# Forming half of a block's weight-gradient products inside the attention forward loop instead of after it

## The chip, the cores and the metric

One Trainium2 chip, one core. The metric is the device time of one execution in microseconds (us). Every version below is correct, except one that is wrong and says so. A program on one core can't be compared with a neighbouring die, so an execution counts as "fast" when it lies within 1.5% of the fastest of the same kernel.

Engines: PE multiplies matrices, DVE and ACT work on vectors, POOL (GpSimd) does some of the elementwise work, SP only issues DMA transfers. SPq is SP's instruction queue. "L351" is a line of that kernel's own file, so the same statement has another line number in another kernel.

## The reference, cut to what matters

A transformer block with adaptive layer norm (2048 tokens, width 512, 32 heads of 16, hidden width 1792), its output and the gradients of nine inputs. Three weight gradients are products over all tokens:

```python
h = _layernorm(x) * (1 + ca) + sa
x = x + ga * attention(h, wqkv) @ wo             # O = attention(...)
h = _layernorm(x) * (1 + cb) + sb                # h2
r = relu(h @ w1 + b1); s = r * r
out = x + gb * (s @ w2 + b2)
# backward, with g = grad_out, gf = g * gb:
# dW2 = s^T gf      dW1 = h2^T dz      dWo = O^T da        (sums over 2048 tokens)
```

The 2048 tokens are four chunks of 512, so each gradient is a sum of four parts, one for each chunk.

## The kernel before

The attention forward pass is a loop of 512 "units": four score products, two exponentials on ACT, one every 0.92 us (945.9 us busy for 1024), four products with V. A unit can't be shorter than its exponentials, about 1.83 us. Chunk c of the dense part (forward and backward of the MLP) is a coroutine. It starts when the heads of its 512 tokens are done and does one small step in each later unit. Chunk 3 has no units left, so it runs after the loop, in the "last stage". There too all weight gradients are formed: "early" products from data of chunks 0 to 2 that were stored to DRAM, then "late" products from chunk 3. The attention backward pass follows.

```python
def load_wB(transposed):                       # (cut)
    w = ffw.tile([P, FC, D], BF, name="wB", tag="wB")
    if transposed:
        for fc in range(FC):                   # 14 transposing loads of w1
            SP.dma_start(out=w[:, fc, :], in_=B_w1[:, fc*P:(fc+1)*P], transpose=True)
    else: ...                                  # one load of w2

def dense_chunk(c, O_c, act):                  # act: chunk 3
    w1_nat = load_wA(False); w1T = load_wB(True)
    g_c = ...; SP.dma_start(out=g_c[:], in_=g_dram[:, ts, :])
    x1_c = ...; SP.dma_start(out=x1_c[:], in_=x_dram[:, ts, :])
    OT = ...;  SP.dma_start(out=OT..., in_=flat(O_c), transpose=True)
    gf_c = ...; POOL.tensor_tensor(gf_c[:], g_c[:], gb_bc..., ALU.mult)
    gfT = ...; SP.dma_start(out=gfT..., in_=flat(gf_c), transpose=True)
    yield 6                                    # wait six units
    for ti in range(4): ...                    # OT @ wo, layer norm   (cut)
    yield 10
    def to_tokens(key, src, f0, f1):           # s or dz, tokens on partitions
        tk = cb.tile([P, 3, 4, P], BF, name="tk", tag="tk", bufs=5)
        SP.dma_start(out=tk..., in_=flat(src[:, f0:f1, :]), transpose=True)
        if act: last[key].append(tk)
        else:   SP.dma_start(out=(s_st if key == "s" else dz_st)[c, f0//3][:, 0:nf], in_=tk[:, 0:nf])
    ...                                        # 14 steps h @ w1; load of w2^T; 14 steps ds   (cut)
    for ti in range(4):                        # gradient through w1: pdh
        for fc in range(FC):
            PE.matmul(pdh[:], dzT[:, fc, ti*P:(ti+1)*P], w1T[:, fc, :], ...)
            if fc % 4 == 3: yield 0
        ...                                    # layer-norm gradient on DVE, first half (cut)
        DVE.tensor_tensor(uq[:], dxn2[:], tq[:], ALU.subtract)        # second half
        DVE.scalar_tensor_tensor(out=dx1_c[:, ti, :], ...)
        DVE.tensor_tensor(proda[:], dx1_c[:, ti, :], a_c[:, ti, :], ALU.mult)
        DVE.tensor_tensor(da_c[:, ti, :], dx1_c[:, ti, :], ga_bc, ALU.mult)
        yield 0
    ...                                        # MLP output with w2; attention gradient (cut)

def fpv(u):                                    # in the forward loop
    ...
    if kt == TT - 1:                           # every 16th unit a group of heads ends
        DVE.tensor_copy(ostage[:], oacc[:])    # frees PE's one accumulator "oacc"

# last stage (cut): gradients
res = dwp["r"].tile([P, 512], BF, name="dwres", tag="dwres", bufs=2)
if nev[0] % 2 == 0: ACT.activation(res[:, 0:w], acc[:, 0:w], AF.Identity)
else:               DVE.tensor_copy(res[:, 0:w], acc[:, 0:w])
SP.dma_start(out=dst, in_=res[:, 0:w])

fill_steps(9)                                  # nine steps of gradient work ...
ffinish(*fdone.pop(0)[1:])                     # ... then O of chunk 3
for w in dense.pop(0): fill_steps(1 + w)       # one gradient step per step of chunk 3
for _ in fill: pass                            # what is left: the tail
```

PE, ACT and DVE run in program order in the forward loop.

## Time and profile before

| | us |
|---|---|
| median of 4 executions (2782.72 to 2788.53) | 2787.55 |
| preparation | to 111 |
| forward loop, 512 units | 111 to 1092.9 |
| last stage | 1092.9 to 1315.4 |
| attention backward, and what follows it | 1315.4 to 2786.6 |

The view of busy time by windows shows the bound. Its rows are the first 128 units without dense work, the units of chunks 0, 1 and 2, and the last stage. Columns: window, its length, busy us (and instruction count) of each engine, granted PE clock (1.00 is full), DMA share, GB/s.

```profile
core 0: us, PE busy (x) PEld busy (x) DVE busy (x) ACT busy (x) POOL busy (x), PEclk, DMA share, GB/s
111.10:344.00 232.90, 215.41 (x1016) 40.06 (x1015) 27.14 (x33) 232.90 (x256) 17.34 (x20) 0.50 0.49 127
344.00:592.00 248.00, 220.03 (x1284) 58.66 (x1280) 90.31 (x186) 234.56 (x255) 34.52 (x39) 0.77 0.37 93
592.00:840.00 248.00, 220.22 (x1286) 58.73 (x1283) 91.73 (x186) 235.77 (x256) 45.22 (x44) 0.77 0.44 106
840.00:1092.90 252.90, 223.37 (x1302) 59.30 (x1303) 92.50 (x186) 240.72 (x260) 45.23 (x44) 0.77 0.48 118
1092.90:1315.40 222.50, 184.06 (x887) 87.57 (x887) 89.15 (x192) 19.39 (x33) 52.29 (x44) 0.91 0.66 163
```

In the loop ACT is the bound: 232.9 of 232.9 us without a chunk, 235 of 248 with one. PE's 220 of 248 us look nearly full, but much of it is slow work: in the 233 us without dense work the granted clock was 0.50, in the chunks' units 0.77. The Trainium skill, "TensorE: Matmul & The Clock Gate", section "What's actually happening", says that the default state is half clock, and that sustained activity of about 3.4 us lifts it. The trace fits: where chunk 0's products begin, at 379 us, the granted clock was 0.50 to 382 us, 0.74 from 382 to 385 and 1.00 from 385 to 388. PE's records fill 215 of the 233 us at 0.50. The first two units after an empty stretch take up to 2.9 us each; they are called cold below. In the last stage PE is the bound, busy 184 of 222 us and idle for 38. (The last stage is counted to the first exponential of the attention backward.)

Three units, one in each chunk, take 6.4 us. The timeline of DVE, then of PE, shows the first (columns: start, duration, engine, line, operation, output and inputs, count, and in brackets the idle time before it with what ended it):

```profile
500.92 1.26 DVE L476 TENSOR_TENSOR uqb<-dxn,tqb 128x512 bf16<-128x512 bf16 x1
502.21 0.75 DVE L477 SCALAR_TENSOR_TENSOR dx_c<-uqb,rstd,g_c 128x512 bf16<-128x512 bf16 x1
503.07 0.43 DVE L480 TENSOR_TENSOR proda<-dx_c,a_c 128x512 bf16<-128x512 bf16 x1
503.53 0.42 DVE L481 TENSOR_TENSOR a_c<-dx_c,modbc 128x512 bf16<-128x512 bf16 x1
503.88 0.68 DVE L590 COPY ostage<-oacc 128x512 f32<-128x512 f32 x1
```

```profile
504.61 0.62 PE L586 MATMUL oacc<-ET,vaug 128*32 128x512 bf16 x4 [3.66 <-DVE ostage L590]
```

PE's next product with V needs the accumulator, and its copy stands behind four DVE operations of the gradient.

### The profile page before, as it was taken

The numbers are of one execution on the slowest core, as the hardware profiler recorded it, in microseconds if no ns is written. First come the engines' busy times: TensorE is split into PE (matmuls) and PEld (weight loads), VectorE is DVE, ScalarE is ACT, GpSimd is POOL, SyncE is SP. The second block draws the span as 40 slices with busy tenths as digits, with TensorE's granted clock in tenths as the row PEclk, the third lists the DMA queues.
The fourth block names the chain that finished last, engine by engine and source line by source line (L and its number), as shares of the span: only waits on it lengthen the run. The fifth ranks groups of instructions, "written<-read, shape, count | busy, mean of one in ns | idle before, by whom it ended". The sixth has DMA issues, their size and how long they took to land.

```text
span 2786.6 us, 47985 instructions
## 1 busy us (share of the span) xinstructions
PE 2453.4 (88%) x17994; PEld 790.8 (28%) x17994; DVE 1710.3 (61%) x2133; ACT 2301.8 (83%) x3531; POOL 366.6 (13%) x326
## 2 busy tenths in 40 slices
PE   6699998898889887799889889889988888989999
PEld 2111122222221222344232332323323233333243
DVE  7101133325333332453798998989889899898873
ACT  4599999999999996101798999989999999999953
POOL 2010010211212022122011010111101011010100
PEclk8655568867885887899799999999999999999999
DMA  8853316344434544784999999999999999999982
GB/s 239 218 153 79 100 48 145 91 120 99 107 95 103 120 128 119 201 191 128 200 190 190 190 189 193 187 189 192 189 187 194 195 189 196 188 186 213 179 249 80
DMA packets 1269550, 449.16 MB, mean 161 GB/s; under 512 B 1187763, under 2 KB 1240503, under 8 KB 1268806
## 3 DMA queue, kind: packets, MB, share of 16 engines
q1 hardware_dynamic: 1262854, 431.71, 77.4%
q10 hardware_dynamic: 6464, 14.40, 1.9%
q8 instruction: 141, 2.31, 0.3%
q14 instruction: 91, 0.75, 0.1%
HBM read 89.81 MB, written 62.94 MB: 55 GB/s over the span
## 4 chain that ended last, share of the span: by engine, by line
PE 39%; ACT 37%; DVE 7%; issue 6%; DMA 5%; SPq 2%; ACTq 0%; POOL 0%; DVEq 0%; POOLq 0%
ACT ET L572 17%; ACT E_u L954 15%; PE psS_u L952 10%; PE accVK L1006 3%; ACT dsT L1065 3%; PE accVK L997 2%; DVE dS_u L966 2%; DMA dsT<-dS_u 2%; PE psST L570 2%; PE pm L436 2%; PE pm L494 2%; PE ptT L987 2%; PE pm L419 2%; PE dqacc L1024 2%; PE dwa L822 2%
## 5 line engine op out<-in xcount | busy, mean ns | idle before, releaser
L966 DVE TENSOR_TENSOR dS_u<-psD_u,E_u 128x1024 bf16<-128x1024 f32 x1024 | 1196.7, 1217 | 145.1 <-PE psD_u L964 72.6
L954 ACT ACTIVATE E_u<-psS_u 128x512 bf16<-128x512 f32 x1790 | 989.3, 617 | 92.7 <-PE psD_u L964 65.0
L572 ACT ACTIVATE ET<-psST 128x1024 bf16<-128x1024 f32 x1024 | 945.9, 1293 | 37.8 <-PE psST L570 37.7
L952 PE MATMUL psS_u<-ik,iq 32*128 32x512 bf16 x1790 | 620.2, 389 | 102.0 <-ACT E_u L954 59.6
L570 PE MATMUL psST<-qt_sb,kt_sb 32*128 32x512 bf16 x2048 | 462.1, 505 | 78.9 <-ACT ET L572 32.1
L964 PE MATMUL psD_u<-iv,ido 32*128 32x512 bf16 x2048 | 410.2, 396 | 14.8 <-DVE dS_u L966 13.7
L586 PE MATMUL oacc<-ET,vaug 128*32 128x512 bf16 x2048 | 270.1, 517 | 13.8 <-DVE ostage L590 13.3
L590 DVE COPY ostage<-oacc 128x512 f32<-128x512 f32 x32 | 22.1, 690 | 351.9 <-PE oacc L586 324.7
L570 PEld LDWEIGHTS <-kt_sb 32*128 32x128 bf16 x2048 | 91.4, 95 | 455.8 <-issue 450.8
L952 PEld LDWEIGHTS <-iq 32*128 32x128 bf16 x2048 | 121.2, 91 | 344.3 <-issue 314.9
L997 PE MATMUL accVK<-dS_u,qz 128*32 128x512 bf16 x2048 | 210.8, 401 | 2.8 <-DVE dS_u L966 0.2
L1006 PE MATMUL accVK<-E_u,dOs_tok 128*16 128x512 bf16 x2048 | 207.3, 395 | 0.0
L1039 POOL TENSOR_TENSOR dQacc<-dQacc,dqtmp 128x512 f32<-128x512 f32 x64 | 81.3, 1270 | 890.8 <-ACT dqtmp L1034 890.8
L964 PEld LDWEIGHTS <-ido 32*128 32x128 bf16 x2048 | 104.8, 91 | 257.3 <-issue 255.0
L1024 PE MATMUL dqacc<-dsT,KS_tok 128*32 128x512 bf16 x2048 | 162.2, 395 | 11.4 <-ACT dsT L1065 11.4
L954 ACT ACTIVATE E_u<-psS_x 128x512 bf16<-128x512 f32 x258 | 159.3, 618 | 0.2 <-PE psD_u L964 0.2
L1065 ACT ACTIVATE dsT<-ptT 128x1024 bf16<-128x1024 bf16 x128 | 133.9, 1046 | 1.1 <-PE ptT L987 1.0
L783 ACT ACTIVATE dwres<-dwa 128x512 bf16<-128x512 f32 (+2 forms) x19 | 10.1, 530 | 132.8 <-DMA out_dram<-dwres 77.0
L586 PEld LDWEIGHTS <-vaug 128*32 128x32 bf16 x2048 | 55.8, 98 | 192.2 <-issue 192.2
L439 DVE SCALAR_TENSOR_TENSOR rT<-pm,rT 128x512 bf16<-128x512 f32 x56 | 38.6, 691 | 113.3 <-PE pm L436 112.2
L952 PE MATMUL psS_x<-ik,iq 32*128 32x512 bf16 x258 | 100.6, 390 | 0.0
L987 PE MATMUL ptT<-identb,dS_u 128*128 128x128 bf16 x1024 | 82.3, 226 | 11.8 <-ACT dsT L1065 11.6
(246 smaller groups left out, 2093.1 us busy)
## 6 DMA issues: line engine op xcount, KB each, us to landing
kt_sb<-qkT_st SPq DMA_DIRECT2D x128, 64.0 KB
wA<-in_B_w_dram SPq DMA_DIRECT2D x4, 1792.0 KB
wB<-in_B_w_dram SPq DMA_DIRECT2D x4, 1792.0 KB
dsT<-dS_u SPq DMA_TRANSPOSE x448
s_st<-tk SPq DMA_DIRECT2D x12, 384.0 KB
dz_st<-tk SPq DMA_DIRECT2D x12, 384.0 KB
slab<-s_st SPq DMA_DIRECT2D x12, 384.0 KB
slab<-dz_st SPq DMA_DIRECT2D x12, 384.0 KB
```

What stands on the lines that cost most here:

```text
L570: PE.matmul(ps[:, hi, :], kt_sb[r:r + 32, kt * P:(kt + 1) * P], qt_sb[r:r + 32, :], start=True, stop=True, tile_position=(r, 0))
L572: ACT.activation(ET[:, 2 * pair:2 * pair + 2, :], ps[:], AF.Exp, scale=SCALE)
L586: PE.matmul(oacc[32 * hq:32 * hq + 32, :], lhsT, ET[:, hq, :], start=(kt == 0), stop=(kt == TT - 1), tile_position=(0, 32 * hq), skip_grou ...
L952: PE.matmul(psS[:], st["q"][r:r + 32, qt * P:(qt + 1) * P], st["k"][r:r + 32, kc * 512:kc * 512 + 512], start=True, stop=True, tile_positi ...
L954: ACT.activation(bst[u][0][:, hq, :], psS[:], AF.Exp, scale=SCALE)
L964: PE.matmul(psD[:, hi, :], st["do"][r:r + 32, qt * P:(qt + 1) * P], st["v"][r:r + 32, kc * 512:kc * 512 + 512], start=True, stop=True, til ...
L966: DVE.tensor_tensor(dS_u[:, 2 * pair:2 * pair + 2, :], psD[:], E_u[:, 2 * pair:2 * pair + 2, :], ALU.mult)
L987: PE.transpose(pt[:, i, :], held["dS"][:, 2 * half + i // 4, kt * P:(kt + 1) * P], identb[:])
L997: PE.matmul(cur["vk"][32 * hq:32 * hq + 32, :], hst[hg]["qz"][:, qt, hq, :], bst[u][1][:, hq, :], start=(qt == 0), stop=False, tile_positi ...
L1006: PE.matmul(acc[32 * hq:32 * hq + DH, :], dOs_tok[:, qt, (hg * 4 + hq) * DH:(hg * 4 + hq + 1) * DH], E_u[:, hq, :], start=False, stop=(qt ...
L1024: PE.matmul(acc[32 * hq:32 * hq + 32, :], KS_tok[:, kc * 4 + kt, h * DH:h * DH + 32], tT[:, :, hq * 4 + kt, :], start=(kt == 0), stop=(kt ...
L1065: ACT.activation(dst, pt[:], AF.Identity)
```

## The change

Intent: the 456 early products need about 95 us of PE in the last stage. Chunks 0 and 1 are finished early enough to form their parts while the forward loop, bound by ACT, leaves PE room. Each part is a chain of four products into one PSUM bank, copied by DVE and stored to DRAM as fp32. Chunk 1's store adds to chunk 0's. Chunk 2's data are stored as before. The last stage loads the sums and adds them when it reads out its accumulators. Also, the second half of the layer-norm gradient of a tile is put off to after the fourth product of the next tile.

```diff
+        def add_chain(c, lag, idx, w, lhs, rhs):
+            def run():
+                acc = mm()
+                for ti in range(4):
+                    PE.matmul(acc[:, 0:w], lhs(ti), rhs(ti), start=(ti == 0), stop=(ti == 3))
+                part = cb.tile([P, 512], F32, name="part", tag="part", bufs=2)
+                DVE.tensor_copy(part[:, 0:w], acc[:, 0:w])
+                if c == 0:
+                    SP.dma_start(out=p_st[idx][:, 0:w], in_=part[:, 0:w])
+                else:
+                    POOL.dma_start(out=p_st[idx][:, 0:w], in_=part[:, 0:w], accum_op=ALU.add)
+            dwq.append((unit[0] + lag, run))
...  (dense_chunk, to_tokens)
+                elif key == "s":
+                    for f in range(nf):
+                        add_chain(c, 5, f0 + f, D, lambda ti, f=f: tk[:, f, ti, :], lambda ti: gf_c[:, ti, :])
...  (the same for dz and O; the gradient's second half becomes finish_dx)
+                    if fc == 3 and rest:
+                        rest.pop()()
...  (forward loop: chains alternate with steps of the chunk, or fill units in which it waits)
+            ripe = dwq and not open_group[0] and u >= dwq[0][0]
+            if wait > 0:
+                wait -= 1
+                if ripe:
+                    next_chain()
+                return
...
+            if ripe and turn:
+                turn = 0
+                next_chain()
+                return
...  (last stage)
                     res = dwp["r"].tile([P, 512], BF, name="dwres", tag="dwres", bufs=2)
-                    if nev[0] % 2 == 0:
-                        ACT.activation(res[:, 0:w], acc[:, 0:w], AF.Identity)
-                    else:
-                        DVE.tensor_copy(res[:, 0:w], acc[:, 0:w])
+                    DVE.tensor_tensor(res[:, 0:w], acc[:, 0:w], parts.pop(j)[:, 0:w], ALU.add)
+                    fetch_part(j + 6)
                     SP.dma_start(out=dst, in_=res[:, 0:w])
...
-                    for t in range(NL):          # 12 early products for each accumulator
+                    for t in range(4):           # now 4
```

## The prediction

> **What bounds the kernel now**, from the busy-by-window view and the timeline. (a) Forward loop, 111 to 1093 us, 512 units of two exponentials: ACT is 92 to 98 of every 100 us busy; a unit without dense work ends every 1.83 us. Chunk work costs more in few places: the first two units after an empty stretch last about 2.86 us with the granted clock near 0.50 (later ones about 1.87), and once per chunk a unit lasts 6.37 us because the copy of the head sum stands on DVE behind the layer-norm gradient. 128 units take 232.8 us without a chunk, 248 with one. (b) Last stage, 1093 to 1314 us: PE is busy 184 of 221 us; 456 early products take 95 us of PE. They interleave one group to one with chunk 3, and 35 us of products (1273 to 1308) follow after chunk 3 is done. (c) Attention backward from 1314: untouched.
>
> **What the change does.** Early products in the last stage fall from 456 to 152: about 63 us less PE (95 x 2/3). They return as 76 chains in the forward loop, each about 0.9 us of PE, a DVE copy of about 0.69 us and a store of 128 to 256 KB; chunk 1's stores accumulate and come from GpSimd (the Trainium skill, "DMA: Bandwidth & Descriptors", SWDGE vs HWDGE: accumulation only there; no run shows its cost yet). The last stage gains 38 loads of sums, and all 38 evacuations become DVE adds instead of 19 on each engine.
>
> **On the critical path.**
> - Forward: chains fall mostly into units whose dense work was waiting; the built order keeps 512 units. Warm chain units cost +0.03 us: +2. Filled gaps avoid about four cold starts of 2 us: -8. The deferred gradient and new alignment shorten the three 6.37 us units: -8 to -11. Against it: only two buffers for sums; in runs of 6 or 7 chains in successive units a store must land within about 3 us. Estimate +0.5 us per such unit for chunk 0, +1.5 for chunk 1: +5 to +20. Net about -6.
> - Last stage: the 35 us tail disappears and W2's products lose their interleave (-7). Chunk 3's own chain remains. Losses: the transpose of O now stands behind six sum loads and the slabs in the SP queue (+10 to 16, mostly repaid by the earlier start of chunk 3's loads); two result buffers make DVE wait for output stores inside chunk 3 (+5 to 8); the row sums are no longer hidden before the tail (+5). Net about -28.
>
> **Prediction:** 2754 us, 8 in 10 within 2722 to 2790. Faster by over 2%: 0.19; within: 0.77; slower: 0.04.
>
> **What would show it.** Forward loop ends within 15 us of 1093; chunk 1's 128 units longer than chunk 0's, DVE copies of sums waiting for DMA; fewer units at clock 0.5. In the last stage PE busy falls by about 60 us but the stage by only 25 to 35, PE idle at the transposed loads (O, h2, w2, da); backward takes the same time.
>
> **What would make it wrong.** Faster: stores land quickly, so the forward loop gains 15 us, and chunk 3, freed of interleaving, runs closer to its DMA chain. Slower: accumulating stores take 8 us or more and stall PE through the chains' single PSUM bank; the SP queue, longer by 76 transfers, delays keys or weights; backward starts later for lack of an operand.

## More of the kernel before

SP's queue is ordered by a scheduler, by what it believes is ready first; once built, the order is fixed.

What SP issued before chunk 1 (its timeline) turned out to matter most. These lines are one stretch of it, with other transfers left out:

```profile
584.97 18.09 SPq L336 DMA_TRANSPOSE wB<-in_B_w_dram  x14
...
615.87 3.87 SPq L363 DMA_TRANSPOSE gfT<-gf_c  x1
...
620.41 3.52 SPq L355 DMA_TRANSPOSE OT<-O_c  x1
```

The fourteen transposing loads of w1 hold SP for 18 us, but they lie between 585 and 603 us. At that time chunk 0 is over and chunk 1 has not begun: 24 units without dense work lie between two chunks (571.5 to 614.4 us on PE). The transpose of O goes out at 620.

In the last stage PE waits little for transfers (view of waits: who waits, for what, us in total, times, longest):

```profile
DVE dwres L785 <- DMA out_dram<-dwres: 27.3, 9, 8.0
...
PE pm L609 <- DMA rrows<-ostage: 10.2, 1, 10.2
...
PE pm L371 <- DMA OT<-O_c: 9.4, 1, 9.4
```

## The result, and the profile after

The changed kernel takes 2812.78 us (median of 4, 2808.77 to 2823.29), beside 2787.55 us before. The ratio is 1.010, 95% interval 1.007 to 1.013: 1% slower, and above the predicted range. Ratios here are the mean time of one kernel's fast runs over that of the other's in the same rounds, so not quite the ratio of the quoted medians.

The profiled execution of after was its slowest (2823 us). Busy time by windows, same rows as before:

```profile
111.20:344.00 232.80, 215.29 (x1016) 40.28 (x1015) 27.15 (x33) 232.80 (x256) 17.30 (x20) 0.50 0.47 124
344.00:593.00 249.00, 221.94 (x1384) 66.43 (x1380) 97.06 (x200) 234.56 (x256) 31.80 (x37) 0.86 0.39 92
593.00:862.00 269.00, 222.94 (x1433) 69.33 (x1431) 111.03 (x222) 236.52 (x256) 75.32 (x80) 0.87 0.59 108
862.00:1126.50 264.50, 219.06 (x1359) 62.37 (x1356) 106.39 (x213) 239.74 (x259) 50.40 (x49) 0.82 0.49 116
1126.50:1341.90 215.40, 134.51 (x583) 58.94 (x583) 97.56 (x211) 9.36 (x15) 53.38 (x45) 0.82 0.65 157
```

Chunk 0's units take as long as before. Those of chunks 1 and 2 take 21 and 12 us more. The forward loop ends at 1126.5 instead of 1092.9 us. The last stage has 50 us less of PE work and is only 7 us shorter: PE now idles 81 us in it instead of 38.

Taking the end of each unit's second exponential from the two traces and sorting the units by length gives the balance of the loop, as the excess over 1.833 us summed over the units of each class:

```
units                     before          after
2.4 to 3.2 us (cold)    29:  25.9 us    16:  15.1 us
over 3.2 us              3:  13.6 us    10:  56.1 us
the rest                      5.6 us          7.4 us
```

So the expected gains came: cold starts fell by 10.8 us, and none of the three 6.4 us units is left. The loss is ten new long units. They are two of 15.5 and 15.7 us (27.5 us over the floor together), six of 4.5 to 7.2 us in which a chain waits (22.5 us), and two others (6.1 us).

The two longest begin chunks 1 and 2. PE, then ACT, at the first (timeline):

```profile
646.14 1.89 PE L395 MATMUL pm<-wo_nat,OT 128*128 128x512 bf16 x4 [12.62 <-DMA OT<-O_c]
```

```profile
648.67 1.94 ACT L622 ACTIVATE ET<-psST 128x1024 bf16<-128x1024 f32 x2 [13.61 <-PE psST L620]
```

PE stands for 12.6 us before the first product with the transposed O; the scores behind it in PE's order are late, and ACT, the bound of the loop, is idle for 13.6 us. Why O is late, SP's timeline shows:

```profile
623.50 5.18 SPq L338 DMA_TRANSPOSE wB<-in_B_w_dram  x4
628.78 1.55 SPq L581 DMA_TRANSPOSE dOT<-dOs_c  x1
630.37 2.58 SPq L338 DMA_TRANSPOSE wB<-in_B_w_dram  x2
...
638.51 3.03 SPq L588 DMA_DIRECT2D d_st<-dltT  x4
641.66 1.77 SPq L378 DMA_TRANSPOSE OT<-O_c  x1
```

The w1 loads are no longer a block at 585 to 603 us. They run from 609.5 to 633 us, between chunk 0's last transfers, and the transpose of O goes out at 641.7. Chunk 0 now ends about when chunk 1's heads do, because its 38 chains took units. The loads wait for chunk 0's w2, whose tile they reuse (SP waits 6.2 us for PE just before them), so they can't start earlier. The 24 empty units that the chains filled had hidden 18 us of SP issue. (The Trainium skill, "Perfetto Trace Analysis", "DMA Instruction — HWDGE (DVE, Sync)", says that such a row ends when the sequencer is free, and that the movement of data is not in it. The trace agrees: this row ends at 643.4, PE goes on at 646.1.)

The waits that grew (view of waits over the whole span):

```profile
PE pm L395 <- DMA OT<-O_c: 46.5, 3, 21.1
...
DVE part L353 <- DMA p_st<-part: 43.1, 14, 5.9
...
DVE dwres L858 <- DMA out_dram<-dwres: 41.8, 20, 9.0
...
PE pm L351 <- DVE part L353: 20.2, 11, 4.5
...
PE dwa L896 <- DVE dwres L858: 15.7, 4, 5.7
...
PE pm L659 <- DMA rrows<-ostage: 15.6, 1, 15.6
...
PE pm L455 <- ACT h2T L415: 13.1, 1, 13.1
```

Line 2: DVE can't copy a sum because both buffers are still being stored, and in line 4 PE waits for that copy. Lines 3 and 5: the same in the last stage with two result buffers. Lines 1 and 6: the 21.1 us for chunk 3's O (9.4 before) and the 15.6 us for the last head's sums (10.2 before). Line 7: chunk 3's transposed h2. Before the change, early products filled this wait (PE ran them to 1147.6 us, when h2 came), and the view of before has no such line. Lines 3 and 5 need care. Before, the read-outs waited longer for output stores, 77.0 us on ACT and 27.3 us on DVE, but the view shows no wait of PE for a read-out. What grew, and what costs, is line 5.

The accumulating stores land like this (issues on POOL; view of one line's instructions):

```profile
L357 POOL DMA_DIRECT2D p_st<-part x38: 851/862/1071, 693.4 to 878.3; - x38
...
DMA to landing us min/median/max: 2.9/4.1/9.1
```

### The profile page after: what moved, and what is told of

Same layout as the page of the kernel before. It is cut to its first block, busy times and chain, and to the rows that moved or that the text cites. A ratio compares the mean times of both kernels' runs of the same rounds, so it can differ in the third digit from the quotient of the medians.

```text
span 2821.5 us, 48292 instructions
## 1 busy us (share of the span) xinstructions
PE 2410.4 (85%) x17994; PEld 783.3 (28%) x17994; DVE 1760.7 (62%) x2228; ACT 2291.6 (81%) x3512; POOL 398.7 (14%) x364
## 4 chain that ended last, share of the span: by engine, by line
PE 38%; ACT 31%; DVE 9%; DMA 8%; issue 6%; SPq 3%; POOL 1%; ACTq 0%; DVEq 0%; POOLq 0%
ACT E_u L1030 14%; ACT ET L622 12%; PE psS_u L1028 10%; PE accVK L1082 3%; ACT dsT L1141 3%; PE psST L620 3%; DVE dS_u L1042 3%; DMA dsT<-dS_u 3%; PE accVK L1073 2%; PE ptT L1063 2%; PE pm L455 2%; PE dqacc L1100 2%; PE pm L472 2%; DMA out_dram<-dwres 2%; PE oacc L636 2%
## 5 line engine op out<-in xcount | busy, mean ns | idle before, releaser
L620 PE MATMUL psST<-qt_sb,kt_sb 32*128 32x512 bf16 x2048 | 417.4, 476 | 65.2 <-ACT ET L622 27.5
L1040 PE MATMUL psD_u<-iv,ido 32*128 32x512 bf16 x2048 | 413.1, 399 | 13.9 <-DVE dS_u L1042 13.2
L636 PE MATMUL oacc<-ET,vaug 128*32 128x512 bf16 x2048 | 253.8, 485 | 7.4 <-DVE ostage L640 6.9
L353 DVE COPY part<-pm 128x512 f32<-128x512 f32 (+2 forms) x76 | 46.0, 605 | 94.8 <-PE pm L351 51.2
L1073 PEld LDWEIGHTS <-qz 128*32 128x32 bf16 x2048 | 55.2, 93 | 125.4 <-issue 123.4
```

Of the source, the lines that this page charges most:

```text
L620: PE.matmul(ps[:, hi, :], kt_sb[r:r + 32, kt * P:(kt + 1) * P], qt_sb[r:r + 32, :], start=True, stop=True, tile_position=(r, 0))
L636: PE.matmul(oacc[32 * hq:32 * hq + 32, :], lhsT, ET[:, hq, :], start=(kt == 0), stop=(kt == TT - 1), tile_position=(0, 32 * hq), skip_grou ...
L1040: PE.matmul(psD[:, hi, :], st["do"][r:r + 32, qt * P:(qt + 1) * P], st["v"][r:r + 32, kc * 512:kc * 512 + 512], start=True, stop=True, til ...
L1073: PE.matmul(cur["vk"][32 * hq:32 * hq + 32, :], hst[hg]["qz"][:, qt, hq, :], bst[u][1][:, hq, :], start=(qt == 0), stop=False, tile_positi ...
```

## The experiments

Four suspects, each with one repair: the w1 loads ahead of O (27.5 us by the unit balance), two buffers for sums (22.5 us), six sum loads and slabs ahead of chunk 3's O (about 12 us), two result buffers (about 15 us). A fifth, PE's wait for h2, has no repair: it is 12.8 to 14.1 us in x1 to x5 too. The rival for all of them: the places share one limit, so that mending one only moves the wait.

Summary of all twelve runs, three timed rounds each. "Loop end" and "last stage" are read from the profiled execution; the kernels x1 to x4 ran together, x5 to x8, x9 to x11, and x12 alone. Chips differ (12, 5, 5, 14), so across these groups compare the ratios. By the 2% rule every one of these kernels counts as the same as before; the intervals say which differences are clear of noise.

| run | us, median | before, same rounds | ratio (95%) | loop end | last stage |
|---|---|---|---|---|---|
| before / after | 2812.8 | 2787.6 | 1.010 (1.007–1.013) | 1092.9 / 1126.5 | 222.5 / 215.4 |
| x1_ot | 2801.4 | 2788.9 | 1.004 (1.002–1.006) | 1112.3 | 218.2 |
| x2_part3 | 2800.6 | 2788.9 | 1.004 (1.002–1.006) | 1109.5 | 217.8 |
| x3_fill3 | 2800.2 | 2788.9 | 1.004 (1.002–1.006) | 1122.5 | 204.1 |
| x4_res5 | 2800.0 | 2788.9 | 1.004 (1.002–1.006) | 1121.5 | 201.6 |
| x5_all | 2763.3 | 2789.2 | 0.991 (0.989–0.994) | 1094.4 | 196.3 |
| x6_plain (wrong) | 2814.1 | 2789.2 | 1.009 (1.007–1.011) | 1125.4 | 217.8 |
| x7_defer | 2775.4 | 2789.2 | 0.995 (0.993–0.996) | 1076.2 | 225.1 |
| x8_head | 2767.9 | 2789.2 | 0.992 (0.991–0.993) | 1093.7 | 199.8 |
| x9_hold | 2778.8 | 2788.5 | 0.997 (0.994–1.000) | 1121.3 | 188.9 |
| x10_hold3 | 2781.2 | 2788.5 | 0.998 (0.995–1.001) | 1118.6 | 196.6 |
| x11_hold3head | 2783.6 | 2788.5 | 0.999 (0.995–1.003) | 1121.9 | 192.7 |
| x12_spread | 2768.2 | 2787.8 | 0.992 (0.991–0.994) | 1116.8 | 190.4 |

### x1_ot: the w1 loads of chunks 0 to 2 moved to after the transpose of h2

```diff
-            w1T = load_wB(True)
+            w1T = load_wB(True) if act else None
...
+            if not act:
+                w1T = load_wB(True)
             yield 10
```

> Only the order of two loads at the start of chunks 0 to 2 changes: the 14 transposed loads of w1 now come after the transpose of O in program order, so 9 of them leave the queue ahead of it. If the sync queue at the chunk boundary is what stalled the two units of 15.5 us (13.7 us over each), they fall to 3 to 8 us, the forward loop ends 12 to 25 us earlier than 1126, and the time is 2787 to 2800. Rival, that transfers are merely slower because there is more DMA traffic: the two stalls stay above 12 us and the time stays at 2805 to 2820.

Measured: the loop ends 14 us earlier, the two units take 6.6 us each instead of 15.5 and 15.7, and the kernel is 11.4 us faster than after. About two thirds of the stall is gone (18 of 27.5 us); the other units over the floor grew by some 4 us together. What is left: the scheduler still put eight of the w1 loads ahead of O, since they were ready. PE's first line of chunk 1 (timeline):

```profile
637.40 1.49 PE L395 MATMUL pm<-wo_nat,OT 128*128 128x512 bf16 x3 [4.08 <-DMA OT<-O_c]
```

### x2_part3: three buffers for sums

```diff
-... name="part", tag="part", bufs=2)
+... name="part", tag="part", bufs=3)
-... name="obf", tag="obf", bufs=2)      # makes room in SBUF
+... name="obf", tag="obf", bufs=1)
```

> Three buffers for the fp32 sums instead of two (room from one buffer fewer for obf). If the two buffers are what made DVE wait 43 us for stores of sums, that wait falls below 15 us, the units over 4 us in runs of chains mostly vanish, the forward loop ends 12 to 20 us earlier and the time is 2793 to 2803. Rival, that the stores are too slow in total (sync and GpSimd queues): the wait stays above 30 us and moves to a later chain, time within 5 us of 2812.

Measured: the loop ends 17 us earlier, and DVE's wait for stores of sums is halved (43.1 to 21.2 us), while the stalls at O are the same (15.5 and 15.6 us). So the two losses are separate places.

```profile
DVE part L353 <- DMA p_st<-part: 21.2, 7, 4.7
...
PE pm L351 <- DVE part L353: 10.7, 6, 3.4
```

### x3_fill3: three gradient steps before chunk 3's O instead of nine

```diff
-            fill_steps(9)
+            fill_steps(3)
```

> The filler before chunk 3's attention output is cut to the three steps of the first job, so the loads of slabs and sums no longer stand ahead of the transpose of O in the last stage. If that order costs what the trace suggests, O's transpose lands 10 to 13 us sooner after the row sums, the last stage is 205 us or less instead of 214, time 2800 to 2806. Rival, that the gap is bound by other loads: under 3 us.

Measured: the last stage is 204.1 instead of 215.4 us, the total 12.6 us less. This changes nothing in the loop, so its loop end of 1122.5 us also says that after's profiled run was some 4 us slow there. (x4_res5, which changes nothing there either, has 1121.5.) The 14 and 17 us of x1 and x2, read against that run, are some 4 us too large; their total times don't have this fault. The number fitted the first job of before, which had nine steps. Now it has three, so nine steps run past it, and the loads that follow it are issued ahead of O.

### x4_res5: five result buffers in the last stage

```diff
-... name="dwres", tag="dwres", bufs=2)
+... name="dwres", tag="dwres", bufs=5)
```

> Five result buffers instead of two in the last stage. DVE waited 41.8 us there for output stores, PE 15.7 us for DVE's adds. If this is on chunk 3's chain, the wait falls below 8 us and the last stage shortens by 12 to 20 us: 2793 to 2801. Rival, that the transposed loads set the pace and DVE waits only in their shadow: under 4 us gained.

Measured: the last stage is 13.8 us shorter, DVE's wait for result stores falls from 41.8 to 0.7 us, and PE's wait for DVE from 15.7 to 1.6 us.

```profile
PE dwa L896 <- DVE dwres L858: 1.6, 2, 1.4
...
DVE dwres L858 <- DMA out_dram<-dwres: 0.7, 2, 0.5
```

### x5_all: the four repairs together

The four edits above, with three result buffers (five don't fit beside three buffers for sums).

> All four repairs at once (transpose of O ahead of the w1 loads for chunks 1 and 2, three buffers for sums, three fill steps, three result buffers). Theory: the four losses are separate places, so the gains add. Alone they gave about -11, -12, -13 and -13 us against the changed kernel; with three result buffers instead of five I take -8 for the last. Expected 2765 to 2775 us, ratio to the kernel before 0.992 to 0.996; forward loop ends 1093 to 1098 (after: 1126.5), last stage 195 to 201 us. Rival: the repairs share the same hidden limit (the SP queue or the chunk's own chain), so what one frees the next wait takes: 2785 to 2800 us, ratio 0.999 to 1.004, with each wait that was removed showing up at another line.

Measured: 2763.3 us. The single gains against after are 11.4, 12.2, 12.6 and 12.8 us, 49 us in sum; together they give 2812.8 − 2763.3 = 49.5 us. The close match is partly luck: it has three result buffers, for which -8 us was expected, in place of the five that gave 12.8, after's four runs lie 14.5 us apart, and against before of the same rounds it is 54 us in sum and 51 together. Within this noise the gains add, so the four losses are largely separate, and the shared limit of the rival, which would have left 2785 us or more, is excluded for them. This version beats both kernels, by 0.9% over before (0.6 to 1.1).

### x6_plain: chunk 1's sums stored plainly from SP (results wrong)

```diff
-                if c == 0:
-                    SP.dma_start(out=p_st[idx][:, 0:w], in_=part[:, 0:w])
-                else:
-                    POOL.dma_start(out=p_st[idx][:, 0:w], in_=part[:, 0:w], accum_op=ALU.add)
+                SP.dma_start(out=p_st[idx][:, 0:w], in_=part[:, 0:w])
```

> The changed kernel, but chunk 1's sums are stored plainly from SP instead of accumulated from GpSimd (the weight gradients come out wrong on purpose, chunk 0's part is lost). Theory: the accumulating store lands later (2.9 to 9.1 us in the changed kernel's trace) than two buffers allow, and so causes most of chunk 1's 26 us of DVE waits: with plain stores chunk 1's waits fall to 8 to 17 us as in chunk 0, forward loop ends 5 to 10 us earlier (1117 to 1121), total 2803 to 2808. Rival: the store's kind does not matter, only the two buffers and the spacing of the chains do (or SP's queue is worse): forward loop within 3 us of 1126, total 2810 to 2818.

Measured: loop end 1125.4, total 2814.1: nothing gained. DVE's waits for stores in chunk 1 were 21.6 us (26.1 with accumulation; chunk 0: 16.1 and 17.0). My theory fell. The kind of store accounts for little; two buffers are too few for a plain store as well. The prediction's split, +0.5 us for a chain unit of chunk 0 and +1.5 us for one of chunk 1, rested on the same idea and falls with it.

### x7_defer: the put-off gradient alone, on the kernel before

```diff
+                    if fc == 3 and rest:
+                        rest.pop()()
...
-                DVE.tensor_tensor(uq[:], dxn2[:], tq[:], ALU.subtract)
-                ...
+                def finish_dx(...):
+                    DVE.tensor_tensor(uq[:], dxn2[:], tq[:], ALU.subtract)
+                    ...
+                rest.append(finish_dx)
                 yield 0
+            rest.pop()()
```

> The kernel before with one part of the change alone: the end of the layer-norm gradient of a tile is put off to after the fourth product of the next tile. Theory of the prediction: the three forward units of 6.4 us (the copy of the head sum stands on DVE behind that gradient) shrink to 2 to 3.5 us, forward loop ends 8 to 11 us earlier (1082 to 1085), total 2777 to 2781, ratio 0.996 to 0.9975. Rival: the long units have another cause or the put-off work only moves the stall to another unit: the loop ends within 3 us of 1093, total 2785 to 2790.

Measured: 2775.4 us, loop end 1076.2. No unit is over 3.2 us. The gain of 14 us (16.7 in the loop of the profiled runs) is larger than expected: 13.6 us from the three units and about 5 us from six cold units fewer (excess 20.6 instead of 25.9 us). The head copy now comes first (DVE, then PE, timeline of the same place as before):

```profile
500.17 0.68 DVE L598 COPY ostage<-oacc 128x512 f32<-128x512 f32 x1
500.77 0.77 DVE L481 TENSOR_TENSOR uqb<-dxn,tqb 128x512 bf16<-128x512 bf16 x1
```

```profile
500.90 0.40 PE L594 MATMUL oacc<-ET,vaug 128*32 128x512 bf16 x4 [0.59 <-DVE ostage L598]
```

So a few moved lines are worth more than half of what all repairs together reach over before (14 of 26 us). Moving the weight gradients, once repaired, comes with the other 12 us (2775.4 to 2763.3, same rounds). No run puts the four repairs on x7_defer without the move, so how much of the 12 us is the move's is not shown.

### x8_head: x5_all, a longer wait for O, and chunk 3's loads asked for earlier

```diff
-            yield 6
+            yield 9 if 0 < c < QC - 1 else 6
...  (g_c, x1_c, gf_c, gfT of chunk 3 made in prefetch(), when chunk 2 is done)
```

> x5_all with two further edits: chunks 1 and 2 wait nine units instead of six between asking for the transpose of O and using it; and chunk 3's gradient and input rows, and the transpose made from them, are loaded when chunk 2 is done, so the last head's sums stand behind them no longer. Theory: in x1 each of the two stalls at the start of chunks 1 and 2 was still 6.6 us long, because six units hold less than the transfer takes, so -8 to -10 us; and in x3 the sums of the last head were asked for about 18 us after they were ready, so -8 to -15 us. Expected 15 to 22 us below x5_all, 2745 to 2757 us. Rival: the start of the last stage is bound by the eight-to-fourteen transposed w1 loads whatever the order, so only the first -8 to -10 come: 2757 to 2766.

Measured: 2767.9 us, not better than x5_all (2763.3). Both theories missed. In the loop, PE's wait for O was all but gone (0.1 us), but units 291 and 380 took 7.6 and 7.1 us instead: in the first the head copy stands on DVE behind its wait of 4.9 us for the transposed h2, in the second PE waits 4.4 us for w2. In the last stage the two waits only changed places (view of waits of that stage, x5_all, then x8_head):

```profile
PE pm L661 <- DMA rrows<-ostage: 15.6, 1, 15.6
...
PE pm L395 <- DMA OT<-O_c: 6.3, 1, 6.3
```

```profile
PE pm L410 <- DMA OT<-O_c: 16.1, 1, 16.1
...
PE pm L676 <- DMA rrows<-ostage: 5.8, 1, 5.8
```

Both pairs add up to 21.9 us. My reading is that whichever of the two stands behind the w1 loads waits for them; x10_hold3 tests it.

### x9_hold: the w1 loads of chunks 1 and 2 held back until half of the forward product is done

A written column makes the loads depend on that moment, so that the scheduler can't move them ahead. (The w1 loads of chunks 0 and 3 also moved later in the program, unheld.)

```diff
+            if held:
+                DVE.memset(w[:, :, 0:1], 0.0)
...
+                if fc == 5:
+                    w1T = load_wB(True, 0 < c < QC - 1)
```

> x5_all, but the fourteen transposed w1 loads of chunks 1 and 2 are held back until the first half of that chunk's forward product is done (an early write of one column of the tile by DVE, which the loads must follow), instead of only standing later in the program. Theory: what is left of the stalls at the start of chunks 1 and 2 (units 278 and 403, 6.8 and 6.6 us) and the long unit 419 (7.2 us, head copy behind DVE's wait for the transpose of h2) all come from w1 loads that still stand ahead in the SP queue. Expected: units 278 and 403 at 2 to 3 us, 419 at 2 to 3 us, forward loop ends 1080 to 1084 (x5_all: 1094.4), total 2750 to 2757. Rival: the transfer of O itself takes longer than the six units whatever stands before it: units 278 and 403 stay over 5 us, forward loop 1090 to 1095, total 2760 to 2766.

Measured: the stalls at O are gone (units 278 and 408 take 2.9 us, and PE no longer waits for O in the loop), which settles their cause: the w1 loads, not O's own transfer. But the loop ends at 1121 us, and the total of 2778.8 us misses both forecasts. Unit 446 takes 19.5 us: the transposed w2 loads now stand behind the w1 loads. SP's timeline, then PE's:

```profile
958.78 7.20 SPq L340 DMA_TRANSPOSE wB<-in_B_w_dram  x5
...
982.72 7.81 SPq L329 DMA_TRANSPOSE wA<-in_B_w_dram  x4
```

```profile
987.10 0.61 PE L476 MATMUL pm<-gfT,wA 128*128 128x512 bf16 x1 [11.43 <-DMA wA<-in_B_w_dram]
```

Two more long units (269 and 399) have another cause. Chunk 1's gradient rows arrive earlier, so GpSimd's product with them meets chunk 0's attention gradient on DVE:

```profile
611.36 4.23 POOL L384 TENSOR_TENSOR gf_c<-g_c,modbc 128x2048 bf16<-128x2048 bf16 x1
```

```profile
612.44 3.19 DVE L584 TENSOR_SCALAR dlt<-delta 128x32 bf16<-128x32 f32 x1
```

The same DVE operation takes 0.18 us when it runs 2.5 us earlier, and ends here with the GpSimd product (615.6). The Trainium skill, "SBUF — State Buffer", "SBUF: two separate sides", describes this: DVE and GpSimd share a pair of ports as an exclusive lock, and the loser blocks for the whole instruction. By the same section not every DVE operation can be caught so: tensor_scalar can, if it runs in a mode with two ports (no view shows whether this one did), and tensor_reduce can't. The times fit that: a TENSOR_REDUCE that ran at 611.72 us, beside the same product, took its usual 0.69 us. No run isolates the lock.

### x10_hold3 and x11_hold3head: the same for chunk 3; and its loads asked for earlier

```diff
-                    w1T = load_wB(True, 0 < c < QC - 1)
+                    w1T = load_wB(True, sT[:, fc, 0:FC] if c > 0 else None)   # copied into w[:, :, 0:1]
```

> x9_hold with the w1 loads of chunk 3 held back in the same way, so that none stands ahead of the last head's sums and of chunk 3's O. Theory: in x5_all PE waits 15.6 us for the last head's sums and 6.3 us for O; in x8_head 5.8 and 16.1 us: about 22 us both times, only dealt out differently, because some ten to twelve of the w1 loads (1.26 us each) stand ahead of one or the other. Held back, the two waits together fall to 8 to 14 us; last stage (196.3 us in x5_all) 184 to 190 us, total 8 to 12 us below x9_hold. Rival: the two waits are bound by the gradient's own load and GpSimd product, which still come first, or the loads held back collide later with the loads of sums and the stores of results: last stage within 3 us of x9_hold's.

> x10_hold3 with chunk 3's gradient and input rows and the transpose of the gradient loaded as soon as chunk 2 is done, as in x8_head. Theory: this takes the wait of SP for GpSimd's product (9.2 us in x3) from ahead of the last head's sums: last stage 3 to 8 us shorter than in x10_hold3. Rival: nothing is gained, since what stands first once the w1 loads are gone is the slowest chain anyway: within 2 us of x10_hold3.

Measured (x10_hold3, view of waits):

```profile
PE dwa L860 <- DMA tk<-sT: 13.4, 1, 13.4
...
PE pm L397 <- DMA OT<-O_c: 7.2, 1, 7.2
```

In both, PE's wait for the last head's sums is gone and that for O is 7.2 us, so the 21.9 us fell to 7.2, even below the 8 to 14 expected. Much of that came in x9_hold already (8.8 and 6.4 us), by program order alone. But a wait of 13 us for the transposes "tk" appeared, and the last stage of x10_hold3 is 196.6 us, against 188.9 in x9_hold; its total is no better (2781.2, 2778.8). The second part of the rival held: the loads collide later, though the stage came out 7.7 us longer and not within 3. In x11_hold3head the stage is 3.9 us shorter than in x10_hold3, as its theory said, but the total gained nothing (2783.6; the ranges of both overlap).

### x12_spread: held back one load for each unit

```diff
+                if 0 < c < QC - 1:
+                    DVE.memset(w1T[:, fc, 0:1], 0.0)
+                    SP.dma_start(out=w1T[:, fc, :], in_=B_w1[:, fc*P:(fc+1)*P], transpose=True)
```

> x9_hold, but the fourteen w1 loads of chunks 1 and 2 are held back one by one, one for each unit of the chunk's forward product, not all together. In x9_hold the stalls at O were gone (2.9 us) but the loads in a block of 17.6 us of SP issue stood ahead of the transposed w2 loads (PE waited 11.4 us and more, unit 446 took 19.5 us) and of stores of sums (units 312, 320). Theory: the SP queue is the shared resource and a block of w1 loads stalls whatever comes behind it; one load of 1.26 us in a unit of 1.83 us lets the others in between: units 278, 403 stay at 3 us, unit 446 falls to 3 to 5 us, 312 and 320 under 5 us, forward loop ends 1082 to 1092, total 2740 to 2755, below x5_all. Rival: SP has no such room in these units either, the loads still push the w2 loads back: forward loop 1100 to 1120, total 2765 to 2780.

Measured: 2768.2 us, loop end 1116.8. Units 324 and 446 take 12.3 and 13.1 us, PE waiting for w2. The rival held, for the loop and for the total: in those units SP has no room either. Since w2 is loaded right after the forward product, a w1 load in any of these units delays it. The total is still only 5 us above x5_all (other rounds, another chip; the intervals of the ratios overlap), though the loop of the profiled run ends 22 us later. Its last stage is 6 us shorter and its backward pass 7 us shorter (1329 and 1336 us, first to last exponential of it); I did not find why the backward pass is shorter there.

## Why the prediction was wrong

- **"Filled gaps avoid about four cold starts of 2 us: -8"** came out at -10.8, partly by luck: x7_defer, which fills no gap, loses 5.3 us of cold starts as well, so some 5 us are left for the gaps. **"shorten the three 6.37 us units: -8 to -11"** had the right mechanism and gave more, -13.6 (x7_defer).
- **The step that failed: "the built order keeps 512 units … Net about -6".** I counted units and the work in them. I did not ask what else used the empty units. They hid the fourteen w1 loads, 18 us of SP issue for each chunk. With the gap filled, the loads stand ahead of the transpose of O: two stalls of 13.7 and 13.9 us, 27.5 us for which the forward sum had no term. x1_ot removed about 18 of it, and in x9_hold only cold units of about 2.9 us are left. The prediction named "the SP queue, longer by 76 transfers" as a danger. But the queue's length was not what showed; what had gone was the time in which it ran unnoticed. The lines for this were in the trace of before, 18.09 us of w1 loads in a gap that the change would fill.
- **"only two buffers for sums … +5 to +20"**: the mechanism was right, the size was just outside, 22.5 us. The split was wrong: the accumulating store is not what costs (x6_plain).
- **"the 35 us tail disappears"**: it did. But the products that moved away had also filled PE's waits in chunk 3: with 50 us less work PE idles 81 us instead of 38. With all four repairs the last stage gained 26 us. That this is close to the predicted 28 is luck, since the 28 already counted the losses that the repairs removed.
- **"+10 to 16, mostly repaid by the earlier start of chunk 3's loads"**: the size was right (11.7 us for O and 5.4 us for the head sums), the repayment did not come. In x8_head an earlier start of chunk 3's loads shortened the wait for the head sums and lengthened that for O by as much. x3_fill3 took back 11 us with one number.
- **"two result buffers … +5 to 8"**: right mechanism, mis-sized. It cost 13 to 14 us (x4_res5: 12.8 in total, 13.8 in the stage). That all 38 read-outs now pass through DVE, so that DVE alone frees PE's six accumulators, is my explanation; no run splits them between two engines again.
- **The sum**: forward +33.6 instead of -6, last stage -7 instead of -28, in the profiled run. The backward pass and what follows took 8 us longer in after's profile; in x1 to x4, which contain the whole change, they took at most 2 us longer than before. x6_plain's profile, also of a 2822 us execution, took 6 us longer. So I put that down to the slow runs and not to the change. "PE busy falls by about 60" measured 50: the early products took 58 us less (95.4 to 37.1), but the granted clock in the stage was 0.82 instead of 0.91, and the late products, as many as before, took 4 us more.

What stays open: why the same backward program took 1329 us in x12_spread's profile and 1336 to 1346 us in the others', and how the w1 loads could be placed without a stall. None of the placements tried (x1, x9, x10, x12) found a free 18 us in SP's queue. The place before the change was such a one, and the chains used it up. Loads issued from another engine's queue were not tried.

## What to carry to other kernels

An empty stretch on one engine may be where another engine's queue does its long work: before filling it, read what the DMA-issuing queue does in that time. Re-tune every constant that counts steps (a number of fill steps, of buffers, of waits) when the steps change size; here three such numbers and one order of loads cost 49 us together, and turned a gain of 0.9% into a loss of 1%. Work that you take out of a stage may have been filling its waits: count the idle time that appears, too. When a change has an independent small part, measure it alone: the put-off gradient by itself gave 14 of the 26 us.

## What the Trainium skill lacked or had wrong

- "DMA: Bandwidth & Descriptors", "Rules for kernel authors", advises to issue a transfer early and to wait on it late. The rule leaves out the limit: each transposing 128x512 load holds the issuing queue for 1.26 us (median of 56 in before), and behind fourteen early ones PE waited long enough for O to make a unit 13.7 us longer. When held back, they delayed the next ones (x9_hold, x12_spread).
- The same page, "Anatomy of one DMA — SWDGE (gpsimd) path", gives a fixed cost of about 2.0 us plus bytes over 436 GB/s. For the 256 KB stores that would be an estimate of 2.6 us. The accumulating stores of 128 to 256 KB landed after 2.9 / 4.1 / 9.1 us (least, median, longest). The page gives no figure for accumulation under load. "SWDGE vs HWDGE vs iDMA" says that accumulation is issued from GpSimd only; each accumulating issue took 0.86 us on POOL (median of 38), for which the page gives no figure.
- "SBUF — State Buffer" describes the lock between DVE and GpSimd, with ratios of slowdown but no durations of such a pair of operations. An example would help: a 0.18 us DVE operation of 128x32 took 3.19 us beside a 4.23 us GpSimd product.
